# A new order of all pieces in a fused attention and feed-forward block, and output tiles in spent weights

## The chip, the cores and the metric

The kernel runs on one core of a Trainium2 chip. The metric is the device time of one execution in microseconds (us), as a median of several runs. All times of single instructions come from one execution that the hardware profiler recorded.

## The reference

One block of a transformer, on 2,048 rows of 640 values in bf16. A layer normalisation feeds two branches, and their sum is added to the input:

```
xn = layernorm(x)
A:  q, k, v = xn @ wqkv, 32 heads of 20
    row s sees the 8 rows s, s-2, ..., s-14
    logits = q . k * 20**-0.5 ; softmax over the 8 ; o = sum attn * v
    A = o @ wo
B:  B = gelu(xn @ w1 + b1) @ w2 + b2        (w1: 640 x 1536)
out = x + A + B
```

## The kernel before

The rows are worked off in four chunks (n = 0 to 3) of 512 rows, each of four blocks (j or bl = 0 to 3) of 128 rows. Everything is cut into 659 *pieces*, and a list written out by hand, `ORDER` (lines 42 to 74), calls them one after the other (lines 765 and 766) under a manual schedule: each engine and each DMA queue executes its own instructions strictly in the order of the list. So the list sets what waits behind what. Waits between engines and for transfers are put in from what each piece reads and writes.

The names of the pieces, with the chunk as the first digit:

- `xn31` normalises block 1 of chunk 3 (ScalarE), `tc31` transposes it with a DMA of the SP queue into the tile `xnT` of the chunk (`do_td`, line 293). `xnT` holds all four blocks, so a projection needs all four transposes.
- `pj302`: projection to q (second digit 0), k (1) or v (2), fifth 2 of the output (`do_pj`, line 330): five matmuls of 128x512. `pc302` copies the result out of PSUM (ScalarE). In chunk 0 smaller pieces `hj`, `hc` and others do this.
- `qk`: VectorE multiplies q by the shifted k, one block j and one half h of the window at a time, into the tile `half`; `pa` adds parts of it up; `lg` sums over a head with matmuls; `cl` copies the logits (ScalarE); `m`, `mx`, `ex`, `ss`, `ri`, `at` are the softmax (VectorE, `ex` on ScalarE).
- `xd10`: a DMA of the SP queue spreads the softmax of chunk 1, block 0, over the partitions of a head (`do_xd`, line 553), 256 KB. `av100` and `av101` multiply it by the shifted v into the same tile `half` (VectorE). `aa10` adds the two halves with an accumulating DMA of the POOL queue (`do_aa`, line 570), 640 KB; in chunk 3 VectorE adds. `ab10` and `ot10` add further on VectorE, into the tile `oT`.
- `f11_4` and `ge1_4`: one of twelve slices of the first feed-forward matmul (five matmuls) and its gelu (ScalarE).
- `o010` to `o014`: the output of chunk 0, block 1, in five pieces: four of feed-forward slices, three pairs of matmuls each, and the last, five pairs, of `oT` with `wo`. `oc01` copies it to an output tile (ScalarE), `od01` adds that to the output in DRAM (POOL queue, accumulating).
- `xp0`, `xp1`, `xp2` write x to the output (SP queue; blocks 0 to 3, 4 to 7, 8 to 14), `xb0` to `xb3` add b2 to it (POOL queue). `ld2` and `ldo` load w2, and wo with b2.

`half` is one tile for all chunks, so the `av` products of a chunk come after `lg` has read its `qk` products. PSUM tiles for projections and feed-forward rotate through six buffers, normalised blocks through three, output tiles through two. The lines that carry the reads the prediction speaks of:

```
def do_td(n, bl):                                            # line 293
    nc.sync.dma_start_transpose(xnT[:, :, bl * P : (bl + 1) * P], tiles["xn", n, bl][:])
def do_pj(n, which, to):                                     # line 330
    xnT = tiles["xnT", n]
...
            rhs=xnT[:, ti, :],
def do_xd(n, j):                                             # line 553
    nc.sync.dma_start(
        ax_view(n)[:, j, :, :],
def do_aa(n, j):                                             # line 570
        nc.gpsimd.dma_start(a, b, accum_op=ALU.add, max_dma_last_dim=CUT)
```

The queue orders that matter, read off the list. SP before: `... xp0 xp2 ldo ld2 tc23 tc20 tc21 tc22 xd00 xd02 xd01 xd03 xp1 xd10 tc30 xd12 xd13 xd11 tc31 tc33 tc32 xd23 ...`. POOL before: `xb3 xb2 xb0 pad02 aa00 aa02 aa01 od00 aa03 aa10 aa11 aa13 od02 aa12 od01 od03 xb1 od12 ...`.

Of the kernel before, what the change touches and what calls it, by code (L numbers as in the profile page):

```python
# [22 lines left out]
NCH = S // CH  # L23
BPC = CH // P
# [21 lines left out]
st13a st13 hj112 hc112 st10 st12 rs1 qk010 rc1 qk000 qk011 hj110 f10_0 ge0_0 hj212 xn13 qk001 xn10 tc13 xn11 hc212  # L46
pa010 hj011 hj010 hc010 f10_11 f10_2 hc110 hc011 qk031 qk021 ge0_11 f10_10 qk020 pa000 su23 f10_6 xn12 ge0_10 qk030
pa020 su21 tc10 tc11 su22 hj200 hc200 f10_3 ge0_3 pa030 pa011 f10_9 tc12 xp0 su20 ng2 sq21 ge0_9 pa021 pj101 pc101
ge0_2 sq23 pj111 pj102 pj114 pc114 xp2 pc102 pj110 pc110 pj104 pa001 ge0_6 pa031 lg0 pc111 cl0 ldo xb3 xb2 pc104 mask
m0 mx0 ex0 pj112 pj103 pc103 pj113 pc113 ss0 ri0 pad11 pj100 pc100 pc112 qk121 qk120 hj211 sq20 hc211 qk101 ld2 pj124  # L50
qk100 sq22 pc124 f10_4 rs2 f11_6 pj121 rc2 ge0_4 pa120 qk110 f11_2 f10_1 ge0_1 pa121 qk111 xn21 pj123 pc123 ge1_6
pa122 pa100 pa110 xn23 f10_7 ge0_7 f11_8 tc23 f11_0 o000 xn20 tc20 tc21 ge1_2 f10_5 ge1_0 xb0 xn22 tc22 qk131 at0 xd00
ge1_8 f11_3 ge1_3 pa111 qk130 su32 pa101 pc121 f10_8 ge0_8 pad02 hj210 f11_5 pa130 pj120 pc120 pj200 pc200 pa112 pj211
pc211 pj210 pj212 pa131 pa102 pc210 hc210 pad12 pa132 lg1 av000 cl1 pj202 ge0_5 pj214 pc202 pj204 av001 aa00 m1 xd02
av021 pad21 av020 xd01 av011 av010 pj220 pj203 su33 ge1_5 su31 su30 ng3 sq33 xd03 av031 o001 pc212 pc203 o002 pc214
sq30 ab00 ot00 aa02 aa01 sq32 sq31 pj213 pc213 xp1 pj221 pj224 rs3 av030 ab02 pj122 pc122 pad22 rc3 ot02 o003 o004
oc00 od00 pj201 mx1 ex1 ss1 ri1 at1 xn31 pc220 xn30 f11_9 o020 o021 o022 o023 xd10 ab01 ot01 pc204 o024 oc02 pc201
aa03 tc30 ab03 f11_4 pc224 o030 o031 o032 pj223 o033 ot03 o034 xn33 av100 f12_3 av101 aa10 xn32 pc223 xd12 av120 xd13
f12_0 f11_11 av130 oc03 pc221 o010 o011 ge2_3 f12_11 o012 ge2_11 ge1_4 ge1_9 xd11 av110 av111 aa11 o013 o014 av121
pj222 pc222 av131 aa13 tc31 tc33 tc32 pj302 pj322 pj300 pc322 pj314 pc314 pj312 ab10 f11_1 ge1_11 ge1_1 f11_7 pj303  # L60
qk201 ot10 qk200 pa200 pc312 ge2_0 pj301 pc301 ab11 pa201 f11_10 pc302 ge1_10 qk211 ot11 od02 qk210 ab13 qk231 ot13
pj324 pc324 pj304 pc304 pa210 qk230 aa12 qk221 ab12 ge1_7 pj311 pa211 oc01 ot12 pa230 od01 f13_2 qk220 pc311 f12_8
pa212 od03 ge3_2 pa220 pc300 o130 pa231 pj313 pa221 o131 o132 o133 o134 oc13 pj310 f13_0 pc303 pc310 ge2_8 xb1 o120
pa202 pa232 pa222 lg2 o121 o122 pad31 pc313 qk300 f13_6 qk311 cl2 m2 qk310 f13_10 qk331 mx2 ge3_6 f13_8 qk330 ge3_0
f13_3 ge3_3 pa310 o123 qk301 o124 ex2 ss2 oc12 od12 f12_7 qk320 ri2 pa311 at2 xd23 pa330 pa300 qk321 f12_4 o110 o111
o112 pa301 o113 ge3_10 f12_10 pa320 pa312 o114 oc11 ge2_10 f12_6 f13_7 ge3_7 ge3_8 ge2_7 o100 o101 pa321 f12_2 xd21
od13 pa331 pa302 pa322 f12_5 o102 o103 ge2_6 ge2_5 o104 pa332 lg3 od11 oc10 od10 pj323 av210 pc323 av211 f12_9 cl3 m3
f13_1 xd22 xd20 ge3_1 pj321 av230 f12_1 ge2_1 aa21 av231 f13_5 ge3_5 av201 av200 aa23 f13_9 mx3 ge2_2 ge2_4 aa20 ab21
f13_4 ge2_9 ot21 ex3 ss3 ri3 ge3_4 f13_11 ge3_11 av220 ab23 o210 o211 at3 xd30 o212 o213 o214 ot23 oc21 od21 av221
aa22 pj320 o330 ab20 pc321 ot20 ge3_9 pad32 pc320 av300 o310 av301 o200 o201 o202 o203 o204 oc20 od20 o311 o230 o231  # L70
xd31 av310 o232 xd32 o233 o234 oc23 o312 o220 o221 o222 av311 aa31 ab22 ot22 o223 o224 od23 oc22 od22 av321 o313 av320
aa32 ab32 ot32 o320 o321 o322 o323 o324 oc32 od32 ab31 ot31 o314 oc31 od31 o300 xd33 o301 o302 o303 aa30 av331 ab30
ot30 o304 oc30 od30 av330 aa33 ab33 ot33 o331 o332 o333 o334 ohi xl oclo ochi ochd
""".split()


# [1 line left out]
def kernel(  # L78
# [16 lines left out]
    nc = tc.nc  # L95
# [19 lines left out]
    outp = ctx.enter_context(tc.tile_pool(name="outp", bufs=2))  # L115
# [3 lines left out]
    wqkv = [wts.tile([P, KT, D], BF16, name=f"w{s}_sb") for s in "qkv"]  # L119
# [60 lines left out]
    mask = consts.tile([H, W, MW], BF16, name="mask")  # L180
# [283 lines left out]
    def do_pa(n, j, k):  # L464

        a, b = ((slice(0, 2), slice(2, 4)), (slice(0, 1), slice(1, 2)), (slice(0, 1), slice(4, 5)))[k]
        kept, gone = (half[:, j, :, :, ts, :].rearrange("p h w t c -> p (h w) t c") for ts in (a, b))
        if k == 0 and j in PA_DMA[n]:
            nc.gpsimd.dma_start(kept, gone, accum_op=ALU.add)
            return  # L470
        nc.vector.tensor_tensor(out=kept, in0=kept, in1=gone, op=ALU.add)  # L471

    def do_lg(n):
# [102 lines left out]

    def do_ab(n, j):
        a, b = (half[:, j, 0, w : w + 2].rearrange("p w t c -> p (w t c)") for w in (0, 2))
        if j in AB_DMA[n]:
            nc.gpsimd.dma_start(a, b, accum_op=ALU.add)  # L580
        else:
            nc.vector.tensor_tensor(out=a, in0=a, in1=b, op=ALU.add)  # L582
# [33 lines left out]
    def do_o(n, bl, pc, parts):  # L616
# [11 lines left out]
        for k, (lhs, rhs) in enumerate(srcs):  # L628
# [80 lines left out]
    for n in range(NCH):  # L709
# [87 lines left out]
```

## Time and profile before

| | us |
|---|---|
| median of 3 runs | 205.92 (205.92 to 206.48) |
| the profiled execution | 206.31 |
| its span, first to last instruction | 204.5 |
| TensorE busy | 200.3 (98%), 1,261 matmuls |
| VectorE busy | 181.6 (89%) |
| ScalarE busy | 127.2 (62%) |
| granted TensorE clock | 1.000 |

A span is counted from the first instruction of the program to the last; all positions below are us from its start. PE is TensorE, DVE VectorE, ACT ScalarE, SP the engine whose queue issues most transfers, POOL the engine that issues the accumulating ones. Matmuls are pipelined: one of 128x512 is listed with 379 ns but the next starts 216 ns later, so a piece of five takes 1.08 us of PE; a pair of 128x512 and 128x128 takes 0.272. VectorE's long products are listed with 1,483 ns and follow each other every 1.40 us.

### The profile page before, as it was taken

To read this page: it belongs to the slowest core of one execution; us is meant where nothing else is said; L and a number is where in the kernel's file an instruction comes from. 1 tells how busy PE (TensorE), PEld (TensorE's weight loads), DVE (VectorE), ACT (ScalarE), POOL (GpSimd) and SP (SyncE) were. 2 spreads that over 40 slices of the span, in tenths; PEclk is the share of its full clock that TensorE was granted. 3 is DMA by queue.
4 is the path that set the end of the run, shared out by engine and by line. 5 is a ranking of instruction groups with operands and counts; after the bars stand their busy time and mean duration, and the time that the engine had idled before them with its cause. 6 is when DMAs were issued, how large, how long until landed. Compare 5 with 4: busy or idle time off the path is not lost.

```text
span 204.5 us, 3231 instructions
## 1 busy us (share of the span) xinstructions
PE 200.3 (98%) x1261; PEld 111.4 (54%) x1261; DVE 181.6 (89%) x226; ACT 127.2 (62%) x246; POOL 34.6 (17%) x49
## 2 busy tenths in 40 slices
PE   8999999999999999999999999999999999999994
PEld 3898565564464555554554554455554455555552
DVE  2699999499998997877999999999989999889991
ACT  5589999999957998846335825474525793111210
POOL 2000000430000243002260050003104224111120
PEclk9999999999999999999999999999999999999999
DMA  6999469899358399999999086005642997962153
GB/s 208 392 396 380 109 213 328 306 256 199 78 116 275 67 171 163 163 144 151 192 190 189 6 90 105 0 0 69 130 107 32 169 189 127 216 101 25 27 67 64
DMA packets 27335, 31.77 MB, mean 155 GB/s; under 512 B 9272, under 2 KB 22072, under 8 KB 27320
## 3 DMA queue, kind: packets, MB, share of 16 engines
q0 software_dynamic: 7408, 12.78, 39.0%
q1 hardware_dynamic: 19600, 18.58, 31.8%
q8 instruction: 10, 0.16, 0.4%
q10 hardware_dynamic: 312, 0.20, 0.3%
q14 instruction: 5, 0.04, 0.1%
HBM read 10.00 MB, written 7.54 MB: 86 GB/s over the span
## 4 chain that ended last, share of the span: by engine, by line
PE 75%; DVE 15%; DMA 5%; ACT 2%; issue 1%; SPq 1%; DVEq 0%; ACTq 0%
PE lo L631 23%; PE hps L595 20%; PE pps L339 17%; PE gps L383 7%; PE hi L633 6%; DVE half L436 5%; DVE half L471 5%; DMA x_sb<-e 3%; DVE half L563 3%; PE gps L352 1%; DVE half L582 1%; DMA x_sb<-in_A_x_dram 1%; PE L L479 1%; DVE oT L586 1%; PE tp L283 1%
## 5 line engine op out<-in xcount | busy, mean ns | idle before, releaser
L595 PE MATMUL hps<-xnT,w_sb 128*128 128x512 bf16 x240 | 55.6, 379 | 0.0
L436 DVE TENSOR_TENSOR half<-qT,kT 128x2560 bf16<-128x2560 bf16 x32 | 46.6, 1483 | 0.1
L631 PE MATMUL lo<-w_sb,hT 128*128 128x512 bf16 x144 | 41.3, 379 | 0.0
L595 PEld LDWEIGHTS <-w_sb 128*128 128x128 bf16 x240 | 23.1, 98 | 26.2
L471 DVE TENSOR_TENSOR half<-half 128x1024 bf16<-128x1024 bf16 (+1 forms) x44 | 36.5, 878 | 0.0
L638 ACT CAST osb<-lo 128x512 bf16<-128x512 f32 x15 | 8.8, 583 | 37.1 <-PE hi L633 18.3
L633 PE MATMUL hi<-w_sb,hT 128*128 128x128 bf16 x144 | 31.5, 219 | 0.0
L611 ACT ACTIVATE hT<-hps,b1T 128x512 bf16<-128x512 f32 x36 | 24.0, 692 | 6.5 <-PE hps L595 5.6
L563 DVE TENSOR_TENSOR half<-vT,x_sb 128x2560 bf16<-128x2560 bf16 x16 | 23.0, 1487 | 3.3 <-DMA x_sb<-e 3.3
L644 POOL DMA_DIRECT2D out_dram<-osb x15 | 13.7, 959 | 71.8 <-ACT osb L639 71.8
L573 POOL DMA_DIRECT2D half<-half x12 | 15.6, 1302 | 56.1 <-DVE half L563 56.1
L563 DVE TENSOR_TENSOR half<-vT,ax 128x2560 bf16<-128x2560 bf16 x16 | 23.0, 1481 | 1.8 <-PE L L479 1.8
L631 PEld LDWEIGHTS <-hT 128*128 128x128 bf16 x144 | 14.1, 98 | 17.2 <-issue 0.4
L631 PE MATMUL lo<-wo,oT 128*128 128x512 bf16 x80 | 23.1, 379 | 0.0
L339 PE MATMUL pps<-xnT,wq_sb 128*128 128x512 bf16 x75 | 18.5, 379 | 0.0
L339 PE MATMUL pps<-xnT,wv_sb 128*128 128x512 bf16 x75 | 18.3, 379 | 0.0
L339 PE MATMUL pps<-xnT,wk_sb 128*128 128x512 bf16 x75 | 18.0, 379 | 0.0
L633 PE MATMUL hi<-wo,oT 128*128 128x128 bf16 x80 | 16.9, 219 | 0.0
L176 ACT ACT_TABLE_LOAD x12 | 15.4, 1283 | 0.9 <-PEq L781 0.7
L633 PEld LDWEIGHTS <-hT 128*128 128x128 bf16 x144 | 14.1, 98 | 1.9
L582 DVE TENSOR_TENSOR half<-half 128x1280 bf16<-128x1280 bf16 x16 | 13.1, 820 | 0.8 <-DMA half<-half 0.8
L403 ACT CAST vT<-pps 128x512 bf16<-128x512 f32 x15 | 8.8, 587 | 6.9 <-PE pps L339 6.9
(91 smaller groups left out, 262.9 us busy)
## 6 DMA issues: line engine op xcount, KB each, us to landing
half<-half POOLq DMA_DIRECT2D x12, 640.0 KB, 6.9
w_sb<-in_B_w_dram SPq DMA_DIRECT2D x4, 960.0 KB, 11.6
out_dram<-osb POOLq DMA_DIRECT2D x15, 160.0 KB, 3.5
ax<-e SPq DMA_DIRECT2D x8, 256.0 KB, 4.1
x_sb<-e SPq DMA_DIRECT2D x8, 256.0 KB, 4.8
out_dram<-b2bc POOLq DMA_DIRECT2D x3, 640.0 KB, 9.7
x_sb<-in_A_x_dram SPq DMA_DIRECT2D x1, 1280.0 KB, 13.7
out_dram<-x_sb SPq DMA_DIRECT2D x2, 640.0 KB, 4.4
```

Of the source, the lines that this page charges most:

```text
L176: nc.scalar.activation(warm[:], nc.const_aps.tensor(0.0, [P, 1], F32), func)
L339: nc.tensor.matmul(ps[:], lhsT=wqkv_p[which][:, ti, to, :], rhs=xnT[:, ti, :], start=(ti == 0), stop=(ti == KT - 1),)
L383: nc.tensor.matmul(ps[:, to - a, :], lhsT=wqkv_p[which][:, ti, to, :], rhs=tiles["xnT", 0][:, ti, pair * 2 * P : (pair + 1) * 2 * P], star ...
L436: nc.vector.tensor_tensor(out=half[:, j, h], in0=q[:, :, at].unsqueeze(1).to_broadcast([P, W // 2, KT, P]), in1=window(k, h, at), op=ALU.mult,
L471: nc.vector.tensor_tensor(out=kept, in0=kept, in1=gone, op=ALU.add)
L563: nc.vector.tensor_tensor(out=half[:, j, h], in0=window(qkv_tile(n, 2), h, cs), in1=ax_view(n)[:, j, ws, :].unsqueeze(2).to_broadcast([P, ...
L573: nc.gpsimd.dma_start(a, b, accum_op=ALU.add, max_dma_last_dim=CUT)
L582: nc.vector.tensor_tensor(out=a, in0=a, in1=b, op=ALU.add)
L595: nc.tensor.matmul(ps[:], lhsT=w1_sb[:, ti, ft * P : (ft + 1) * P], rhs=tiles["xnT", n][:, ti, :], start=(ti == 0), stop=(ti == KT - 1),)
L611: nc.scalar.activation(hT, tiles["hps", n, ft][:], ACT.Gelu_apprx_tanh, bias=b1T[:, ft : ft + 1], scale=1.0)
L631: nc.tensor.matmul(lo[:], lhsT=lhs, rhs=rhs[:, 0:CH], start=first, stop=last)
L633: nc.tensor.matmul(hi[:, 0 : D - CH], lhsT=lhs, rhs=rhs[:, CH:D], start=first, stop=last)
```

## The change

The list is new from the piece after `st13a` on; the lead-in before it is the same. No piece is added or taken away, and each engine has as many instructions as before. Besides, the output tiles of chunk 3 and of block 0 of chunk 2 no longer come from the two rotating buffers: they lie in the tile of the weights of v (`wqkv[2]`), which no projection reads any more by then. Two options that were empty (`AB_DMA`, `PA_DMA`) are gone with their branches.

Cut to the rows of the list that the prediction speaks of:

```diff
-ge0_2 sq23 pj111 pj102 pj114 pc114 xp2 pc102 pj110 pc110 pj104 pa001 ge0_6 pa031 lg0 pc111 cl0 ldo xb3 xb2 pc104 mask
...
-pc211 pj210 pj212 pa131 pa102 pc210 hc210 pad12 pa132 lg1 av000 cl1 pj202 ge0_5 pj214 pc202 pj204 av001 aa00 m1 xd02
-av021 pad21 av020 xd01 av011 av010 pj220 pj203 su33 ge1_5 su31 su30 ng3 sq33 xd03 av031 o001 pc212 pc203 o002 pc214
-sq30 ab00 ot00 aa02 aa01 sq32 sq31 pj213 pc213 xp1 pj221 pj224 rs3 av030 ab02 pj122 pc122 pad22 rc3 ot02 o003 o004
-oc00 od00 pj201 mx1 ex1 ss1 ri1 at1 xn31 pc220 xn30 f11_9 o020 o021 o022 o023 xd10 ab01 ot01 pc204 o024 oc02 pc201
-aa03 tc30 ab03 f11_4 pc224 o030 o031 o032 pj223 o033 ot03 o034 xn33 av100 f12_3 av101 aa10 xn32 pc223 xd12 av120 xd13
-f12_0 f11_11 av130 oc03 pc221 o010 o011 ge2_3 f12_11 o012 ge2_11 ge1_4 ge1_9 xd11 av110 av111 aa11 o013 o014 av121
-pj222 pc222 av131 aa13 tc31 tc33 tc32 pj302 pj322 pj300 pc322 pj314 pc314 pj312 ab10 f11_1 ge1_11 ge1_1 f11_7 pj303
...
+hc110 hc011 qk000 qk030 tc10 qk021 qk020 f10_11 ge0_11 f10_3 f10_10 xn11 tc11 su22 hj200 xn12 tc12 xp1 ldo f10_9 xp0
+xb0 ge0_3 pa000 pa010 hc200 ge0_10 su20 f10_2 ge0_2 ge0_9 su23 su21 ng2 f10_6 ge0_6 ld2 qk031 sq23 pa020 pj114 pj101
...
+pa131 tc20 pj200 ge0_4 pc200 pa102 pj212 xp2 pj211 pj210 su30 pc212 su32 ng3 sq33 pa132 lg1 pj202 av000 pc202 xd03
+pc210 cl1 av001 sq30 pj203 xd02 av020 aa00 sq31 av021 pc211 aa02 pj201 av031 av011 av010 aa01 pj122 pj213 pj223 pc201
+o001 ab00 ot00 pc213 sq32 rs3 rc3 pj221 av030 xn33 pj204 pj214 pc214 m1 aa03 pad21 pc223 o002 o003 o004 oc00 ab02 od00
+mx1 ex1 f12_3 pj222 pc222 o020 o021 o022 o023 ot02 o024 oc02 ss1 ri1 at1 pc204 ab01 ot01 xn31 f12_11 o030 xn30 o031
+o032 o033 ab03 pc122 xd13 ot03 av130 pc203 o034 f12_8 xd10 av101 av100 oc03 tc33 pad22 o010 xn32 f12_0 ge2_0 xd11
+av110 xd12 av121 aa10 av111 ge2_11 pad31 tc30 aa11 f11_9 ge2_3 av131 aa13 tc31 od02 pc221 o011 o012 o013 o014 av120
+ab10 ge2_8 tc32 pj313 pj303 pc303 pj300 pj322 pc322 qk201 ot10 qk200 aa12 pj220 pj310 pc310 pj304 ab11 pc300 pc313
...
+    def out_tile(n, bl):
+        if (n, bl) == (2, 0) or n == NCH - 1:
+            return wqkv[2][:, bl if n == NCH - 1 else BPC, :]
+        return outp.tile([P, D], BF16, tag="osb", name="osb")
     def do_oc(n, bl):
-        osb = outp.tile([P, D], BF16, tag="osb", name="osb")
+        osb = out_tile(n, bl)
...
     def do_oclo():
-        osb = outp.tile([P, D], BF16, tag="osb", name="osb")
+        osb = out_tile(*last)
```

The queue orders after. SP: `... xp1 ldo xp0 ld2 xd01 xd00 tc21 tc22 tc23 tc20 xp2 xd03 xd02 xd13 xd10 tc33 xd11 xd12 tc30 tc31 tc32 xd22 ...`. POOL: `xb0 pad02 aa00 aa02 aa01 aa03 od00 aa10 aa11 aa13 od02 aa12 od01 od03 xb1 od13 xb2 od12 xb3 od11 ...`.

More of the change, by code (lines that the diff above doesn't have):

```diff
@@ L34 @@
 BY_DMA = ((0, 1, 2, 3), (0, 1, 2, 3), (0, 1, 2, 3), ())
-AB_DMA = ((), (), (), ())
-PA_DMA = ((), (), (), ())
 CUT = 2560
@@ L45 @@
 hc100 xn03 tp03 tc03 pk hj202 rc02 xn02 tp02 tc02 gc4 hj201 hc201 hj111 st11a st10a hc111 st12a hj012 hc012 st11 hc202
-st13a st13 hj112 hc112 st10 st12 rs1 qk010 rc1 qk000 qk011 hj110 f10_0 ge0_0 hj212 xn13 qk001 xn10 tc13 xn11 hc212
-pa010 hj011 hj010 hc010 f10_11 f10_2 hc110 hc011 qk031 qk021 ge0_11 f10_10 qk020 pa000 su23 f10_6 xn12 ge0_10 qk030
-pa020 su21 tc10 tc11 su22 hj200 hc200 f10_3 ge0_3 pa030 pa011 f10_9 tc12 xp0 su20 ng2 sq21 ge0_9 pa021 pj101 pc101
-ge0_2 sq23 pj111 pj102 pj114 pc114 xp2 pc102 pj110 pc110 pj104 pa001 ge0_6 pa031 lg0 pc111 cl0 ldo xb3 xb2 pc104 mask
@@ L50 @@
[L50 to L53, printed above, removed]
-pc211 pj210 pj212 pa131 pa102 pc210 hc210 pad12 pa132 lg1 av000 cl1 pj202 ge0_5 pj214 pc202 pj204 av001 aa00 m1 xd02
@@ L60 @@
-pj222 pc222 av131 aa13 tc31 tc33 tc32 pj302 pj322 pj300 pc322 pj314 pc314 pj312 ab10 f11_1 ge1_11 ge1_1 f11_7 pj303
[L61 to L73, printed above, removed]
+st13a st10 hj112 hc112 hj212 st12 st13 qk001 rs1 rc1 f10_0 ge0_0 xn10 qk011 hj011 qk010 hj010 xn13 tc13 hc010 hj110
@@ new lines @@
+hc110 hc011 qk000 qk030 tc10 qk021 qk020 f10_11 ge0_11 f10_3 f10_10 xn11 tc11 su22 hj200 xn12 tc12 xp1 ldo f10_9 xp0
+xb0 ge0_3 pa000 pa010 hc200 ge0_10 su20 f10_2 ge0_2 ge0_9 su23 su21 ng2 f10_6 ge0_6 ld2 qk031 sq23 pa020 pj114 pj101
+pj111 pc111 pad02 pa001 pa030 pc114 pc101 pj112 pc112 pj104 pa021 sq21 pj110 pc110 pa011 hc212 pa031 lg0 cl0 mask m0
+pc104 mx0 ex0 ss0 ri0 pj100 pc100 pj103 pj102 pc102 pj113 f10_4 hj210 pc113 pc103 pad11 qk121 qk101 qk110 sq22 at0
+sq20 xd01 hc210 xd00 rs2 pj123 pc123 f11_0 ge1_0 rc2 qk120 qk130 f11_6 ge1_6 qk100 qk111 pa100 pj121 pa110 xn21 pc121
@@ new lines @@
+tc21 xn22 tc22 f10_8 ge0_8 pa120 pa111 pa121 xn20 pj120 qk131 pa112 f10_7 pc120 ge0_7 xn23 f11_3 tc23 f11_8 ge1_8
+f11_5 ge1_5 pa130 f10_1 ge0_1 pa101 su33 su31 hj211 hc211 pad12 f10_5 ge0_5 o000 ge1_3 pj124 f11_2 ge1_2 pc124 pa122
+pa131 tc20 pj200 ge0_4 pc200 pa102 pj212 xp2 pj211 pj210 su30 pc212 su32 ng3 sq33 pa132 lg1 pj202 av000 pc202 xd03
+pc210 cl1 av001 sq30 pj203 xd02 av020 aa00 sq31 av021 pc211 aa02 pj201 av031 av011 av010 aa01 pj122 pj213 pj223 pc201
+o001 ab00 ot00 pc213 sq32 rs3 rc3 pj221 av030 xn33 pj204 pj214 pc214 m1 aa03 pad21 pc223 o002 o003 o004 oc00 ab02 od00
@@ new lines @@
+mx1 ex1 f12_3 pj222 pc222 o020 o021 o022 o023 ot02 o024 oc02 ss1 ri1 at1 pc204 ab01 ot01 xn31 f12_11 o030 xn30 o031
+o032 o033 ab03 pc122 xd13 ot03 av130 pc203 o034 f12_8 xd10 av101 av100 oc03 tc33 pad22 o010 xn32 f12_0 ge2_0 xd11
+av110 xd12 av121 aa10 av111 ge2_11 pad31 tc30 aa11 f11_9 ge2_3 av131 aa13 tc31 od02 pc221 o011 o012 o013 o014 av120
+ab10 ge2_8 tc32 pj313 pj303 pc303 pj300 pj322 pc322 qk201 ot10 qk200 aa12 pj220 pj310 pc310 pj304 ab11 pc300 pc313
+pj301 pc301 f11_10 pa200 ge1_10 pc220 ot11 pc304 qk211 qk210 ab13 f11_11 pj302 f13_2 ge3_2 pc302 f11_4 pa210 ge1_4
@@ new lines @@
+pj224 oc01 pc224 f13_0 od01 ot13 qk231 qk230 od03 ab12 pa211 f11_1 ge1_1 qk221 ot12 pa230 pj312 pj311 pc311 qk220
+f11_7 pa201 ge1_7 o130 pj314 pa220 pa202 pc312 ge1_9 pa231 pa221 ge1_11 o131 o132 o133 o134 oc13 xb1 od13 pad32 pj324
+pc324 pa212 o120 xb2 pa222 pa232 lg2 pc314 qk300 f12_10 qk320 o121 cl2 m2 mx2 ex2 ge2_10 qk331 o122 o123 o124 oc12
+f12_4 ge2_4 f13_6 qk310 qk321 qk311 f13_7 ss2 ri2 f12_5 od12 pa310 pa320 o110 f12_2 f13_8 ge3_8 pa311 o111 o112 qk330
+o113 o114 oc11 f12_7 o100 ge3_6 at2 xd22 qk301 xd21 pa321 o101 o102 pa300 pa330 pa322 ge2_2 ge2_7 f13_10 pa301 o103
@@ new lines @@
+xb3 f12_6 ge2_6 o104 pa331 ge3_7 pa312 pa302 ge2_5 od11 oc10 od10 f13_3 ge3_3 pa332 lg3 av210 f13_11 cl3 f12_9 ge3_11
+av211 f13_4 ge3_4 ge3_10 m3 f13_5 xd23 av230 av231 f12_1 ge2_1 xd20 av200 f13_1 ge3_1 mx3 pj323 av201 ge3_0 pc323 aa21
+ab21 ot21 av220 pj320 o310 ge3_5 o330 ex3 ss3 ge2_9 pj321 pc321 o210 o211 o212 o213 ri3 at3 xd30 av221 xl aa23 aa20
+aa22 o214 oc21 od21 ab20 ot20 f13_9 ab23 pc320 o200 o201 o202 o203 o204 oc20 av300 o311 o230 o231 o232 o233 ot23 o234
+oc23 od20 o312 av301 xd31 av310 av311 aa31 o220 o221 o222 ab22 ot22 o223 o224 od23 ge3_9 o313 oc22 xd32 av321 av320
@@ L74 @@
+o320 o321 o322 o323 aa32 ab32 od22 ot32 o324 ab31 ot31 o314 aa30 ab30 ot30 oc32 od32 oc31 od31 xd33 av330 av331 aa33
+ab33 ot33 o300 o301 o302 o303 o304 oc30 od30 o331 o332 o333 o334 oclo ohi ochi ochd
 """.split()
@@ L467, in do_pa @@
         kept, gone = (half[:, j, :, :, ts, :].rearrange("p h w t c -> p (h w) t c") for ts in (a, b))
-        if k == 0 and j in PA_DMA[n]:
-            nc.gpsimd.dma_start(kept, gone, accum_op=ALU.add)
-            return
         nc.vector.tensor_tensor(out=kept, in0=kept, in1=gone, op=ALU.add)
@@ L578, in do_ab @@
         a, b = (half[:, j, 0, w : w + 2].rearrange("p w t c -> p (w t c)") for w in (0, 2))
[L579 to L582, printed above, removed]
+        nc.vector.tensor_tensor(out=a, in0=a, in1=b, op=ALU.add)
     def do_ot(n, j):
```

## The prediction

> **What bounds the kernel now.** I read the busy shares first, then TensorE's waits, then the chain, then the timelines of the queues. The page:
>
> ```profile
> PE 200.3 (98%) x1261; PEld 111.4 (54%) x1261; DVE 181.6 (89%) x226; ACT 127.2 (62%) x246; POOL 34.6 (17%) x49
> PE   8999999999999999999999999999999999999994
> DMA  6999469899358399999999086005642997962153
> PE 75%; DVE 15%; DMA 5%; ACT 2%; issue 1%; SPq 1%; DVEq 0%; ACTq 0%
> ```
>
> TensorE never rests between its first microseconds and its last. A busy PE proves little, so I took the gaps between starts: outside the lead-in only one place is more than a quarter of a microsecond over the usual step, the logits of chunk 2. The timeline of PE there:
>
> ```profile
> 127.13 0.39 PE L479 MATMUL L<-half,head_of 128*32 128x512 bf16 x2
> 127.70 0.61 PE L479 MATMUL L<-half,head_of 128*32 128x512 bf16 x6 [0.18 <-DVE half L471]
> ```
>
> Two starts 0.57 us apart instead of 0.06: PE waited 0.51 us for VectorE's last addition. So the chain crosses to VectorE and to DMA (15% and 5%) only because both run neck and neck with PE up to here. The kernel is bound by TensorE, and an order alone can win at most this 0.51 us. It can lose wherever PE is sent to something that is not there yet. The two places to look at are VectorE's and the DMAs'. The timelines of SP and POOL around the only stretch where DMA is full for long (slices 14 to 21, 72 to 112 us), with what is known of the last two transposes:
>
> ```profile
> 85.31 0.55 SPq L554 DMA_DIRECT2D x_sb<-e  x1
> 85.97 2.12 SPq L295 DMA_TRANSPOSE xnT<-xn  x1
> 88.18 2.66 SPq L554 DMA_DIRECT2D x_sb<-e  x3
> 90.89 7.97 SPq L295 DMA_TRANSPOSE xnT<-xn  x3
> ...
> 92.57 1.20 POOL L573 DMA_DIRECT2D half<-half  x1 [10.55 <-DVE half L563]
> 99.64 1.20 POOL L573 DMA_DIRECT2D half<-half  x1 [5.87 <-DVE half L563]
> ...
> DMA to landing us min/median/max: 4.6/6.1/7.6
> ...
> 94.00:96.00 2.00, 2.00 (x13) 0.94 (x11) 1.16 (x1) 1.18 (x3) 0.00 (x0) 1.00 1.45 54
> 96.00:100.00 4.00, 4.00 (x29) 2.11 (x27) 3.55 (x3) 2.25 (x4) 0.36 (x1) 1.00 1.03 190
> ...
> 101.10 1.24 PE L339 MATMUL pps<-xnT,wv_sb 128*128 128x512 bf16 x5
> 102.18 0.59 PE L339 MATMUL pps<-xnT,wq_sb 128*128 128x512 bf16 x2
> ```
>
> The landing row is for the transposes issued at 93.3 and 96.85: 7.6 us after the first (100.9) and 4.6 us after the second (101.4). The two rows by windows end with the DMA share and GB/s: from 94 to 96 the engines hold packets and move a quarter of what they do after. The last row is `pj302`, the first projection of chunk 3, which needs all four transposes: it found them with 0.8 us to spare.
>
> **The change part by part.** Each engine has the same instructions, the twelve table loads of ScalarE included, so nothing is added up but waits. The sum is made against the profiled execution (206.31: span 204.5 and 1.8 around it); it lies 0.39 above the median, and I put the difference on the median, 205.92.
>
> *PE's places.* With 1.08 us for a slice or projection and 0.272 for a pair of output matmuls, I added up what stands ahead of each point in both lists. The four logits, `o004`, `o204` and `o334` come out at the same microsecond (35.5, 64.5, 127.2, 152.9, 77.4, 173.8, 199.4 in both). What moved lies between them. The first projection of chunk 3 moved most. Before, `f11_11`, `f11_4`, `pj220` and `pj224` stood ahead of it and now do not; `f12_8` was behind and is ahead. That is three pieces less: PE comes to `pj313` at 102.18 - 3 x 1.08 = 98.94.
>
> *The four transposes of chunk 3.* They wait on SP behind the first spread of chunk 1, and that behind the softmax. Is the softmax earlier? Its exponential starts at 81.02 once ScalarE has copied `o004` and loaded a table (copies 78.85 and 79.33, load 79.61). Both stand as before, and VectorE's `mx1` ends about 80.1, which is soon enough: the shuffle of VectorE's pieces gains nothing, and the spread is issued at 85.3 again. Then SP sends the same eight transfers, four spreads and four transposes, one transpose early and three last in both lists. In the profile that took until 101.4. Bounds: in an idle stretch (52 to 59 us) each of four transposes landed 2.4 us after its issue; the last can't be issued before `xn32`, which follows the copy of `o034` on ScalarE (91.3 + 0.7 + 0.2 for `pad22` + 0.9 = 93.1), so 95.5 at best, no wait. At worst they share the engines with all four accumulations of chunk 1 and land with the third of these, about 107. I take 101.4, the row of this very set of transfers. PE then starts `pj313` about 0.1 us after it (at the logits VectorE's addition ended at 127.65 and PE went on at 127.70), at 101.5: a wait of 2.56 us. PE has no idle time behind it to win this back.
>
> *VectorE up to the logits of chunk 2.* Its idle times before: 1.46 (exponential), 0.26 (`ab03`), 1.23 and 1.29 (spreads). Now `ot02` stands ahead of the wait for the exponential but ends in the same 82.1; `aa03` is issued right behind `av030`, no longer behind `od00`, so 0.26 goes; the first spread is awaited until 89.4 as before; the third is issued earlier, so 1.29 may go. But the product that completes the first accumulation is third, not second, so `aa10` is issued at 93.8, not 92.57; with the 7.8 us it took, `ab10` starts about 101.6 instead of 102.06. Then the same 25.5 us of work: the last addition ends by 127.2, while PE comes to `lg2` at 127.13 + 2.56. So the 0.51 us goes. VectorE then waits for the copy of `pj314` (it stands on ScalarE behind that of `o134`, which PE ends at 125.1 + 2.56; four copies of 1.8 us in all follow) and starts chunk 3's products at about 129.6; 25.0 us later (127.63 to 152.60 before) it has the last addition at 154.6, against PE at `lg3` at 153.26 - 0.51 + 2.56 = 155.3. No further wait, but the margin is 0.7.
>
> *The rest, at nothing, with its cover.* Moving `xb2` and `xb3` from 39 us behind `xb1` (126 us on) puts 1.1 MB beside the spreads of chunk 2; these landed at 152 at the latest and the products start at 153.7. The spreads `xd01`, `xd00` go ahead of the transposes of chunk 2 (softmax done at 47.7), the last of which then is issued at 56.4 (`xn23` is ready at 55.0 in ScalarE's new order) and lands 2.4 us later, 1.3 before PE wants `pj200` (60.1). `xp2` now stands on SP ahead of `xd03` and `xd02`: it and two spreads are the same 1.6 MB that landed in 9.0 us from 58.26, so from 57.6 by 66.6, and `av020` comes at 67.9; a delay below 0.9 would be hidden under ScalarE's table load. The tile change: before, an output copy had to wait for the landing two blocks earlier, but the waits of line 638 end with PE (18.3 and 8.9 us) or with nothing shown, never with a DMA, and the closest landing (196.3) lies 1.5 us ahead of its copy (197.8); so nothing is gained, and no projection to v is left that could be hurt. After `lg3`, VectorE's results come 1.3 us or more ahead of PE's use. PSUM is freed at the nearest 0.2 us ahead, as before.
>
> Sum: 205.92 + 2.56 - 0.51 = 207.97, so **208.0**.
>
> [...] While `aa10` moves, I counted the trace's DMA packets: in 97 to 99 us 79 and 64 of 2,560 bytes a microsecond, and beside them only 71 and 69 of a transpose's 256 bytes; right behind, from 100.0, 991 of these passed in 0.93 us. [...]
>
> **The rivals.**
> *Crawl.* The pass in the gap between `aa10` and `aa11` is what let the transposes land by 101.4: these two were issued 7.07 us apart. Now three products lie between them (3 x 1.40 = 4.2 us), and an accumulation's packets take 3.6 us (96.41 to 99.98), so the gap is 0.6 us or none. Three transposes are 1,920 packets; 525 had passed by 94.6, and at the rate of issue (640 in 1.2 us) some 700 more do by 95.6, where `aa10` now starts. Beside it 407 passed, so some 300 are left for the next accumulation: landing at 103.5 to 107, about 105, a wait of 6.1. Time: 205.92 - 0.51 + 6.1 = 211.5. Against it: 300 packets need no more than a gap of 0.3 us.
> *Hidden (the other side, not slower).* `aa10` starts 1.2 us later, and at 991 packets in 0.93 us the 1,920 need 1.8 us. It decides if the last lands before 98.9. Then only 0.51 is left: 205.4. Against it: SP needed 2.0 to 3.5 us to issue each of the three, and the standstill of 94 to 96 may recur.
> *VectorE's margin.* A late `xd02` or the 0.7 at `lg3` give 0.2 to 1.0 more on any case.
>
> **How the numbers follow.** A change below 0.3% (0.6 us) can't be told from none. The forecast (206.6 to 210) has 0.50, crawl (over 210) 0.22, hidden 0.25 (205.3 to 206.5, mostly same), a run below 205.3 0.03, since the floor is 205.41. The forecast's own range is 206.6 to 210. Four in five lie from 205.2, the floor with its scatter, to 212.5, inside the crawl. Faster 0.03, same 0.23, slower 0.74.
>
> **What would show it.** The profile after should have PE idle before line 339's first chunk-3 matmul, near 99 us, ended by the DMA `xnT<-xn`; no gap at `lg2`; VectorE idle near 127 to 130, before a product of q and k; the spread issued at 85.3. I am wrong if the transposes land before 98.9, if the softmax of chunk 1 is earlier, or if PE has a second gap: at `pj200`, at `lg3`, or where a product is waited for.

## The result and the profile after

The changed kernel takes 209.11 us in the median (208.31 to 209.88, 6 runs), beside 205.94 for the kernel before on the same chip: 1.0152 times, 95% interval 1.0136 to 1.0168. The profiled execution took 209.24 (span 207.2), 2.93 more than that of before. The forecast, 208.0, was 1.1 us short, with the right sign and the time inside its range. Executions at a lower granted clock, or more than 1.5% above the fastest of the same kernel, are left out of all ratios.

The page of the changed kernel: busy shares, TensorE and DMA by slices, the chain by engines.

```profile
PE 199.1 (96%) x1239; PEld 111.2 (54%) x1261; DVE 181.4 (88%) x226; ACT 126.7 (61%) x246; POOL 34.6 (17%) x49
...
PE   8899999999999999999699999999999999999994
...
DMA  6999399983867299899997093738382997972253
...
PE 77%; ACT 10%; DMA 8%; issue 2%; DVE 1%; SPq 0%; another core or an unknown queue 0%; ACTq 0%
```

Slice 20 (98 to 104 us) has a 6 where before had a 9: TensorE stood still there. (22 records of matmuls are missing from this trace: a group that shows x4 where a piece has five is such a hole, and the busy share can't be set against that of before.) The chain has lost VectorE, 15% before and 1% now, and has ScalarE at 10%. From the list of waits (engine, line, waited for: total, times, longest):

```profile
DVE half L434 <- PE L L474: 3.9, 1, 3.9
...
PE pps L337 <- DMA xnT<-xn: 1.7, 1, 1.7
...
ACT xn L264 <- DMA xnT<-xn: 0.9, 1, 0.9
...
PE hps L587 <- ACT hT L603: 0.7, 1, 0.7
```

And the timelines of the changed kernel at those places (start, length, what; in brackets the idle time before it and what ended it):

```profile
55.73 0.92 ACT L264 ACTIVATE xn<-x_sb,nmr,rstd 128x640 bf16<-128x640 bf16 x1 [0.93 <-DMA xnT<-xn]
...
57.28 1.24 PE L587 MATMUL hps<-xnT,w_sb 128*128 128x512 bf16 x4 [0.68 <-ACT hT L603]
...
86.44 1.19 SPq L549 DMA_DIRECT2D x_sb<-e  x2
87.75 2.01 SPq L293 DMA_TRANSPOSE xnT<-xn  x1
89.80 1.24 SPq L549 DMA_DIRECT2D x_sb<-e  x2
91.14 5.75 SPq L293 DMA_TRANSPOSE xnT<-xn  x3
...
94.89 1.20 POOL L568 DMA_DIRECT2D half<-half  x1 [12.97 <-DVE half L558]
99.10 1.19 POOL L568 DMA_DIRECT2D half<-half  x1 [3.01 <-DVE half L558]
...
100.11 0.22 PE L625 MATMUL hi<-wo,oT 128*128 128x128 bf16 x1
102.04 1.25 PE L337 MATMUL pps<-xnT,wk_sb 128*128 128x512 bf16 x4 [1.71 <-DMA xnT<-xn]
...
130.23 0.61 PE L474 MATMUL L<-half,head_of 128*32 128x512 bf16 x8
130.73 2.90 DVE L434 TENSOR_TENSOR half<-qT,kT 128x2560 bf16<-128x2560 bf16 x2 [3.88 <-PE L L474]
```

Read by TensorE's starts, beyond the usual step: 1.88 us before `pj313` (100.1 to 102.0), where the forecast put 2.56; no wait inside the eight logits of chunk 2, where before had 0.51; and 0.84 before `f10_5` at 57.28, which the forecast did not have. That one starts on ScalarE: `xn23` waited until 55.7 for a transpose, its buffer being one of three, and the gelu behind it (`ge1_8`) held the PSUM buffer that `f10_5` takes. With 0.39 in the unchanged lead-in (first weights landed 0.38 later in this execution) the sum is 0.39 + 0.84 + 1.88 - 0.51 = 2.60 of a span that is 2.7 longer.

### The profile page after: what moved, and what is told of

Its sections match the earlier page's. It is cut to its first block, busy times and chain, and to the rows that moved or that the text cites. A ratio compares the mean times of both kernels' runs of the same rounds, so it can differ in the third digit from the quotient of the medians.

```text
span 207.2 us, 3202 instructions
## 1 busy us (share of the span) xinstructions
PE 199.1 (96%) x1239; PEld 111.2 (54%) x1261; DVE 181.4 (88%) x226; ACT 126.7 (61%) x246; POOL 34.6 (17%) x49
## 4 chain that ended last, share of the span: by engine, by line
PE 77%; ACT 10%; DMA 8%; issue 2%; DVE 1%; SPq 0%; another core or an unknown queue 0%; ACTq 0%
PE lo L623 24%; PE pps L337 20%; PE hps L587 18%; PE hi L625 7%; DMA xnT<-xn 6%; PE gps L381 6%; DMA wq_sb<-in_A_wqkv_dram 3%; ACT xn L264 2%; ACT L174 1%; PE gps L350 1%; ACT qT L401 1%; ACT hT L603 1%; PE L L474 1%; ACT trash L229 1%; ACT osb L635 1%
## 5 line engine op out<-in xcount | busy, mean ns | idle before, releaser
L623 PE MATMUL lo<-w_sb,hT 128*128 128x512 bf16 x140 | 40.5, 379 | 0.1
L466 DVE TENSOR_TENSOR half<-half 128x1024 bf16<-128x1024 bf16 (+1 forms) x44 | 35.8, 876 | 0.0
L568 POOL DMA_DIRECT2D half<-half x12 | 15.1, 1258 | 65.1 <-DVE half L558 62.9
L635 ACT CAST osb<-lo 128x512 bf16<-128x512 f32 x11 | 6.4, 585 | 22.4 <-PE lo L623 13.0
L641 POOL DMA_DIRECT2D out_dram<-osb x11 | 10.8, 1009 | 53.4 <-ACT osb L636 44.7
L337 PE MATMUL pps<-xnT,wq_sb 128*128 128x512 bf16 x72 | 17.6, 380 | 0.2
L337 PEld LDWEIGHTS <-wk_sb 128*128 128x128 bf16 x75 | 8.6, 118 | 9.3 <-issue 2.4
```

The source lines that it names most:

```text
L337: nc.tensor.matmul(ps[:], lhsT=wqkv_p[which][:, ti, to, :], rhs=xnT[:, ti, :], start=(ti == 0), stop=(ti == KT - 1),)
L623: nc.tensor.matmul(lo[:], lhsT=lhs, rhs=rhs[:, 0:CH], start=first, stop=last)
```

## The experiments

Theory: the new order loses at two places, where `xn23` waits for a buffer and where PE comes three pieces too early for the last transpose of chunk 3. Rivals: the loss is given back elsewhere, belongs to the tiles, or is DMA time that no order sets. Ratios are to the kernel before on the same chip, with 95% intervals.

**One cure: `xn23` in a buffer of its own.**

```diff
     def xn_tile(n, bl):
+        if (n, bl) == (2, 3):
+            return get(("xn", n, bl), lambda: outp.tile([P, D], BF16, tag="osb", name="xn23"))
         return get(("xn", n, bl), lambda: lnp.tile([P, D], BF16, tag="xn", name="xn"))
```

> The changed kernel, but the last normalised block of chunk 2 (`xn23`) gets a tile of its own (an output buffer that is not yet used at 55 us), so it no longer shares a buffer with the block whose transpose `tc21` landed at 55.65. Theory (the 0.84 us that PE stood still before `f10_5` came from ScalarE waiting in `xn23` for that landing): `xn23` starts near 54.8, the gap at 57 us goes, everything behind it, the first spread of chunk 1 included, comes some 0.6 to 0.8 us earlier, and the time is 209.1 - 0.7 = 208.4. Rival 1 (given back): the gap goes, but the last transpose of chunk 3 does not land earlier, so PE waits 0.7 us longer at `pj313`: 209.1. Rival 2 (another cause): the gap before `f10_5` stays at 0.8: 209.1.

Measured: 208.63, ratio 1.0102 (1.0068 to 1.0136). In its timeline ScalarE goes into `xn23` without idle time, although `tc21` landed as late as before (55.85), and PE has no gap at `f10_5`:

```profile
54.88 0.94 ACT L266 ACTIVATE xn<-x_sb,nmr,rstd 128x640 bf16<-128x640 bf16 x1
```

So the buffer was the cause, and the time is 0.2 us from the expected 208.4. The wait at `pj313` stayed (1.39). The first rival falls: the last transpose came earlier by as much as PE, and more.

**The other cure: three pieces ahead of `pj313`.**

```diff
-ab10 ge2_8 tc32 pj313 pj303 pc303 pj300 pj322 pc322 qk201 ot10 qk200 aa12 pj220 pj310 pc310 pj304 ab11 pc300 pc313
-pj301 pc301 f11_10 pa200 ge1_10 pc220 ot11 pc304 ...
-pj224 oc01 pc224 ...
+ab10 ge2_8 tc32 pj220 pc220 f11_10 ge1_10 pj224 pc224 pj313 pj303 pc303 pj300 pj322 pc322 qk201 ot10 qk200 aa12 pj310
```

> The changed kernel with six pieces (`pj220` and its copy, `f11_10` and its gelu, `pj224` and its copy: 3 x 1.08 us of PE work that needs no transpose of chunk 3) moved from behind `pj313` to in front of it. Theory (PE came three pieces too early for the last transpose, nothing more): the wait at `pj313` (1.88) goes, since PE comes there at 103.4 with the landing at 101.9; the gap before `f10_5` stays; time 209.1 - 1.9 = 207.2. Rival (the wait only moves: the projections that now stand right behind wait for the transposes or for PSUM buffers, or VectorE, which gets chunk 3's projections no earlier, ends later): a gap of 1 us or more at another place behind 101 us, time 208.5 to 209.1.

Measured: 207.78, ratio 1.0084 (1.0047 to 1.0120). The timeline goes from one projection into `pj313` (line 337, `wk_sb`) with no idle time:

```profile
101.98 1.24 PE L337 MATMUL pps<-xnT,wv_sb 128*128 128x512 bf16 x5
103.06 1.24 PE L337 MATMUL pps<-xnT,wk_sb 128*128 128x512 bf16 x5
```

The transpose landed at 101.78, as before the cure; no new gap appears, and that at `f10_5` is still there (0.77). The profiled execution, 206.96, is where the theory put it (207.2); the median is 0.6 above the theory.

**The same step in the old list.** Three pieces go from in front of chunk 3's first projection to behind it; nothing else of the change is in.

```diff
-f12_0 f11_11 av130 oc03 pc221 o010 o011 ge2_3 f12_11 o012 ge2_11 ge1_4 ge1_9 xd11 av110 av111 aa11 o013 o014 av121
-pj222 pc222 av131 aa13 tc31 tc33 tc32 pj302 pj322 pj300 pc322 pj314 ...
+f12_0 av130 oc03 pc221 o010 o011 ge2_3 o012 ge1_4 ge1_9 xd11 av110 av111 aa11 o013 o014 av121
+av131 aa13 tc31 tc33 tc32 pj302 pj322 pj300 pc322 f11_11 f12_11 ge2_11 pj222 pc222 pj314 ...
```

> The kernel before, with five pieces (`f11_11`, `f12_11` and its gelu, `pj222` and its copy: 3 x 1.08 us of PE work) moved from in front of the first projections of chunk 3 to behind them, so that PE comes to `pj302` at 98.9 instead of 102.18; nothing else of the change. Theory (the wait at chunk 3's first projection is the price of three pieces less in front): PE waits there for the last transpose (landing 101.4) for 2.5 us, the 0.51 us at the logits of chunk 2 goes, time 205.9 + 2.5 - 0.5 = 207.9. Rival (hidden): the transposes land earlier too or the wait is won back, 205.4 to 206.2.

Measured: 210.11, ratio 1.0187 (1.0146 to 1.0227). The timeline:

```profile
99.16 0.22 PE L633 MATMUL hi<-wo,oT 128*128 128x128 bf16 x1
102.58 0.60 PE L339 MATMUL pps<-xnT,wq_sb 128*128 128x512 bf16 x2 [3.20 <-DMA xnT<-xn]
```

PE came 3.4 us too early, and the 0.51 at the logits went. The step alone costs as much as the whole change (the intervals overlap), since the transpose landed at 102.49 here and not at 101.41. Hidden it is not. But the expected 207.9 was missed by 2.2 us: 0.9 of it is the longer wait, and 0.7 lies between the profiled execution (209.39) and the median.

**The tiles alone, the order alone.** The first is the old list with `out_tile`, the second the new list with the old line:

```diff
 # the order alone
-        osb = out_tile(n, bl)
+        osb = outp.tile([P, D], BF16, tag="osb", name="osb")
```

> The old list of pieces with the new place of the output tiles (chunk 3 and block 0 of chunk 2 in the spent weights of v). Theory (an output copy ends with PE, not with the landing of an earlier output): the same time as before, 205.9 within 0.4. Rival (the tiles save waits for landings, or make copies wait for the last projections to v): 0.5 us or more away from before, on either side.

> The new list of pieces with the old two rotating output tiles. Theory (the whole difference is the order): the changed kernel's time, 209.1 (1.012 to 1.018 times before), with the gaps at `f10_5` (0.8) and `pj313` (1.9). Rival (the new order needs the new tiles, since outputs of chunk 2 and 3 follow each other faster in it): 209.6 or more, with ScalarE's output copies ended by DMA landings near 150 or behind 195 us.

Measured: tiles alone 206.19, ratio 1.0006 (0.9988 to 1.0023), no difference. Order alone 210.74, ratio 1.0240 (1.0211 to 1.0268): the rival holds. It is slower than with the new tiles, and the theory (209.1) is wrong. Its timeline has a third gap:

```profile
184.84 0.58 ACT L638 CAST osb<-lo 128x512 bf16<-128x512 f32 x1 [6.54 <-DMA out_dram<-osb]
...
185.47 0.38 PE L631 MATMUL lo<-w_sb,hT 128*128 128x512 bf16 x1 [1.67 <-ACT osb L638]
```

The copy `oc23` waits until an earlier output has landed, and PE waits 1.83 us for the copy before `o220`. So the tiles are worth nothing in the old order and 1.8 us in the new one.

**Both cures.**

> The changed kernel with both cures: a tile of its own for `xn23`, and three pieces of PE work (`pj220`, `f11_10`, `pj224` with their copies and gelu) ahead of `pj313`. Theory (the two waits are the whole loss, and the 0.51 us at the logits of chunk 2 is a true gain): no gap over 0.3 us behind the lead-in, 205.4 to 206.0, that is 0.997 to 1.000 times before. Rival (something that no gap of PE shows, or a new wait, holds the changed order back): 206.8 or more, as the two single cures, which came out 0.3 to 0.6 us less well than their gaps, would let one think.

Measured: 206.84, ratio 1.0036 (1.0020 to 1.0052). The profiled execution, 206.10 with a span of 204.2, has no gap of PE over 0.3 behind the lead-in, and its chain is:

```profile
PE 95%; DMA 1%; ACT 1%; issue 1%; DVE 0%
```

That execution has the theory's time within 0.1 us. The other eleven lie between 206.45 and 208.35, and the median is the rival's (206.8 or more). So the two waits are most of the loss (1.0152 to 1.0036), and about 0.7 us stays that this profile does not show.

**Where does the time of the transposes go?** In the trace a 16 KB packet of the queue called instruction passes ten times, about once per 250 PE instructions (weight loads and matmuls). At 26, 53 and 95 us one fell among the 256-byte packets of transposes; there 19, 22 and 17 of these were under way at once for 1 to 2 us each, and little else moved (35 GB/s in 27 to 28, 36 in 54 to 55, 57 in 95 to 96). Such packets are called held below, and the stretch a hold. The stretches 52 to 56 of the changed kernel (engine columns, granted clock, then DMA share and GB/s), with this packet at 53.14:

```profile
52.00:53.00 1.00, 1.00 (x7) 0.42 (x5) 1.00 (x2) 1.00 (x3) 0.00 (x0) 1.00 1.17 205
53.00:54.00 1.00, 1.00 (x6) 0.45 (x5) 1.00 (x1) 1.00 (x2) 0.00 (x0) 1.00 2.26 90
54.00:55.00 1.00, 1.00 (x6) 0.47 (x5) 1.00 (x2) 0.81 (x2) 0.00 (x0) 1.00 0.22 36
```

The packets that start in 53 to 54 fill the DMA engines 2.26 times over while 90 GB/s pass, then 36. If this is what made `tc21` late, moving the packet must move the hold. Three kernels move it by idle matmuls in the warm-up, whose results nothing reads:

```diff
         do_warm(3, P)
+        do_warm(12, 32)     # on the kernel after; and on the kernel before
...
-        do_warm(WARM, CH)
+        do_warm(WARM - 4, CH)
         do_warm(3, P)
+        do_warm(40, 32)     # on the kernel after, the longer one
```

> The changed kernel with 12 more idle matmuls of 32 columns in the warm-up ahead of the first piece, where PE waits for its first weights anyway; nothing else is touched. In the trace a 16 KB packet of the instruction queue passes once per some 256 PE instructions; at 53.14 and at 94.73 it fell among the 256-byte packets of transposes, and at both places some 20 packets of all engines then took 1 to 2 us. 24 more PE instructions bring these packets some 2 us earlier (near 51 and 92.7), where only 2,048-byte packets are under way. Theory (the instruction packet among the transposes holds the DMA engines): no packet is held near 53 and near 95, `tc21` lands near 54 instead of 55.65 and the gap before `f10_5` goes (0.7), `tc32` lands 1 us or more earlier against PE's course, so that the wait at `pj313` falls from 1.9 to under 1: 207.0 to 208.0. Rival (the hold belongs to the transposes, or to the start of an accumulation, or is chance): holds at the same places as before, time 209.1 within 0.3.

> The kernel before with 12 more idle matmuls of 32 columns in the warm-up and nothing else; it asks where the instruction packets fall, not for time. Theory (an instruction packet among 256-byte packets of transposes holds the DMA engines for 1 to 2 us): if the packet at 93.76 moves out of the transposes, no packets are held near 94 to 96, and the transposes issued at 93.3 and 96.85 land 1 us or more before 100.9 and 101.4; if it moves onto other transposes (those of chunk 2, 53 to 59 us), the hold appears there. The time stays (205.9 within 0.4), for PE did not wait for them. Rival (the hold belongs to the start of the first accumulation): held near 94 to 96 wherever the packet falls.

> The changed kernel with a longer warm-up in front of the first piece (6 idle matmuls of 512 columns in place of 10, and 40 of 32 columns): some 72 more PE instructions, which should bring each packet of the instruction queue some 7 us earlier, to about 46 and 88 in place of 53 and 95, both ahead of transposes. Theory (an instruction packet among transposes holds the DMA engines): no packets are held near 53 nor near 95; `tc21` takes 3.3 us in place of 4.6 and the gap before `f10_5` goes; `tc32` lands 1.5 us sooner after its issue, at 5 to 5.7 in place of 7.2, and the wait at `pj313` falls below 1.0. Time 207.0 to 207.8, plus what the longer warm-up costs in the lead-in (0 to 0.5). Rival (the hold near 95 belongs to the transposes or to the first accumulation): it stays, with a wait of 1.4 to 2.1 at `pj313`, and the time is 208.3 to 209.3.

Measured. Twelve matmuls on the kernel after: ratio 1.0123 (1.0048 to 1.0197), so nothing follows from the time. The packet went from 53.1 to 47.6, no packets were held there, `tc21` took 3.25 us in place of 4.57, and the gap at `f10_5` was gone; but the later packet stayed among the transposes (95.3), and so did the hold. (Its profile is of an execution of 211.53 us; the kernel with forty repeats what it shows at 53.) Twelve on the kernel before: ratio 1.0020 (1.0004 to 1.0035); the packet at 93.8 did not move, nor the hold: inconclusive for its question. Forty: 208.92 and 208.98 us, two of four executions, without a ratio; the rival's time. Both packets moved, to 44.8 and 90.0. The same stretch as above now reads:

```profile
52.00:53.00 1.00, 1.00 (x7) 0.47 (x5) 1.00 (x1) 1.00 (x2) 0.00 (x0) 1.00 0.83 183
53.00:54.00 1.00, 1.00 (x7) 0.41 (x6) 1.00 (x2) 1.00 (x2) 0.00 (x0) 1.00 0.92 175
54.00:55.00 1.00, 1.00 (x6) 0.49 (x5) 1.00 (x2) 1.00 (x3) 0.00 (x0) 1.00 0.74 167
```

The hold at 53 is gone and with it the gap at `f10_5`, without touching a buffer; the hold at 95 is gone too; and a new one stands at 90.3 to 90.8, among the packets of `tc33`, which took 5.0 us in place of 4.2. So the hold follows the packet, and it is what made `tc21` late. Its price at `pj313` was misjudged, though: that wait stayed at 2.03, and `tc32`, with no packet held, still took 6.1 us. Something else sets its landing.

**What sets the landing of the last transpose.** Read from the traces (us):

```
kernel                       aa10 issued  landed    tc32 issued  landed
before                          92.57     100.33       96.85     101.41
after                           94.89     101.34       94.70     101.90
xn23 in a buffer of its own     94.32     100.72       94.36     100.89
both cures                      93.76     100.09       93.77     100.09
old list, three behind          92.83     101.42       94.83     102.49
forty idle matmuls              95.19     101.33       95.73     101.82
aa10 behind aa11               100.48     109.30       95.86      99.35
```

In all rows but the last, `tc32` lands 0 to 1.1 us behind `aa10`, whenever it was issued (4.6 to 7.7 us before it lands). The packets of the changed kernel show how: in 98 to 100 us 57 and 67 of the transpose's packets a microsecond passed beside 72 and 72 of the accumulation's, 156 of its 640 up to 100.42; once the last packet of `aa10` had started then, the other 484 passed in 0.98 us. The last row is the test, one issue moved on POOL:

```diff
-av110 xd12 av121 aa10 av111 ge2_11 pad31 tc30 aa11 f11_9 ...
+av110 xd12 av121 av111 ge2_11 pad31 tc30 aa11 aa10 f11_9 ...
```

> The changed kernel with one issue on POOL moved: the first accumulation of chunk 1 (`aa10`) behind the second (`aa11`), so that both start near 99 to 101 us and none runs while the last transposes of chunk 3 do. It asks when `tc32` lands. In all traces so far the last transpose lands 0 to 1.2 us behind `aa10` (90 to 102 us: landings 100.1 to 103.4), whether it was issued 2.5 or 7.4 us earlier, and whether packets were held or not. Theory (the last transpose goes packet for packet beside `aa10` and so ends with it): without it `tc32` lands 2.4 to 4.5 us after its issue, at 97.2 to 99.3, PE finds it there and the wait at `pj313` (1.9) goes. VectorE then waits for `aa10` until about 107, some 5 us, and PE for VectorE at the logits of chunk 2, by 2 to 4 us: time 209 to 211. Rival (held packets, or the transposes' own rate, set the landing): `tc32` lands at 101 or later as before, wait 1.4 to 2.0 at `pj313`, time 211 to 213.

Measured: 214.82, ratio 1.0386 (1.0322 to 1.0450). `tc32` landed 3.5 us after its issue though packets were held in its way (16, behind the instruction packet at 95.8), and PE went into `pj313` without a wait. How long the last two transposes took to land in the changed kernel and in this one, the timeline of PE and VectorE, and the stretches behind the waits (granted clock third from the end):

```profile
DMA to landing us min/median/max: 4.0/5.6/7.2
...
DMA to landing us min/median/max: 3.5/3.8/4.2
...
100.85 0.22 PE L624 MATMUL hi<-wo,oT 128*128 128x128 bf16 x1
100.91 1.24 PE L336 MATMUL pps<-xnT,wk_sb 128*128 128x512 bf16 x4
...
109.39 0.82 DVE L573 TENSOR_TENSOR half<-half 128x1280 bf16<-128x1280 bf16 x1 [7.11 <-DMA half<-half]
...
131.77 0.38 PE L473 MATMUL L<-half,head_of 128*32 128x512 bf16 x1 [2.61 <-DVE half L465]
133.58 0.38 PE L473 MATMUL L<-half,head_of 128*32 128x512 bf16 x1 [1.43 <-DVE half L465]
...
134.00:136.00 2.00, 1.40 (x6) 0.34 (x7) 2.00 (x3) 0.59 (x2) 0.00 (x0) 0.60 0.83 138
136.00:138.00 2.00, 1.87 (x5) 0.70 (x5) 1.97 (x4) 1.97 (x3) 0.00 (x0) 0.54 0.00 0
138.00:140.00 2.00, 2.00 (x17) 1.12 (x15) 1.93 (x4) 0.74 (x1) 0.00 (x0) 1.00 0.00 0
```

The theory on the landing holds. The time is above what it gave, and above the rival's too: VectorE waited 7.1 us for the late accumulation, not 5; PE stood idle 4.5 us at the logits of chunk 2; and right behind these waits the granted clock was 0.60 and 0.54, with matmuls of 128x512 every 427 ns in place of 216. From the last output matmul ahead of the logits to the first one behind them PE took 8.89 us, beside 1.79 in the changed kernel. With 7.1 for that, 0.5 in the lead-in and the 1.88 gone at `pj313`, the sum is 5.7 of a span that is 5.8 longer.

**Two tries at a faster kernel.** Both cures with the longer warm-up, and the old list with one output piece ahead of the logits that waited:

```diff
-pa202 pa232 pa222 lg2 o121 o122 pad31 pc313 ...
+pa202 pa232 pa222 o121 lg2 o122 pad31 pc313 ...
```

> The changed kernel with both cures (own tile for `xn23`, three pieces ahead of `pj313`) and the longer warm-up. The two cures alone came out at 206.84, 0.7 us above what their profile (206.1, no gap of PE) says. Theory (in the other executions the held transposes come later still and PE waits after all): without holds the median falls to the profile's level, 205.8 to 206.3. Rival (the 0.7 has nothing to do with held packets): 206.7 to 207.3.

> The kernel before with one piece moved: `o121` (three pairs of output matmuls, 0.81 us of PE work that waits for nothing) stands ahead of the logits of chunk 2 and no longer behind them. Theory (the 0.51 us in those logits is the only wait of PE behind the lead-in that an order can remove): PE has the 0.51 us of work in hand, the softmax starts 0.3 us later, which nothing waits for; 205.4 to 205.7, 0.9965 to 0.9985 times before. Rival (the softmax of chunk 2, 0.3 us later, is what chunk 2's spreads and VectorE's products wait for up to `lg3`, where the gain is given back): 206.0 to 206.4, with a gap of 0.3 to 0.5 at `lg3`.

Measured: 207.02, ratio 1.0046 (1.0029 to 1.0063), and 206.99, ratio 1.0058 (1.0038 to 1.0078). The first speaks against the idea that the packets held near 53 and 94 make the 0.7 us of the two cures: both holds are gone from its profile (one of 17 packets stands at 89.3), and the median is no better. The second was to win 0.5 and lost. Its logits of chunk 2 have no wait, but those of chunk 3 have two:

```profile
14.49 1.68 DVE L211 BATCH_NORM_STATS2 stats<-x_sb 128x6 f32<-128x320 bf16 x4 [1.54 <-DMA x_sb<-in_A_x_dram]
...
154.25 0.55 PE L478 MATMUL L<-half,head_of 128*32 128x512 bf16 x3
155.03 0.59 PE L478 MATMUL L<-half,head_of 128*32 128x512 bf16 x5 [0.23 <-DVE half L470]
155.55 0.63 PE L338 MATMUL pps<-xnT,wv_sb 128*128 128x512 bf16 x2
```

From the first of these logits to the next piece PE took 1.30 us, beside 0.55 for the same eight without a wait and 1.12 for those of chunk 2 in the kernel before: 0.57 was won there and 0.75 lost here. So VectorE takes the whole gain back 25 us later, as its rival said. The time is above the rival's too (206.0 to 206.4), and the rest of the loss was not found. The profiled execution alone has another 1.39 us at 29 us, ahead of anything that was edited; it begins with the input x, for which VectorE waited until 14.49 (first line). No version beat the kernel before.

## Why the prediction was right, and where it was not

*The bound.* Right. Every gap that mattered was TensorE waiting, and with both waits cured the profiled span came to 204.2, beside 204.5 before. The 0.51 us at the logits of chunk 2 went, as forecast (0.57, measured from the first logit to the next piece).

*PE's place at `pj313`.* Right. The count of three pieces gave 98.94; the trace has 100.16, later by the 1.2 us that PE had lost before (0.39 and 0.84). Taking the three pieces back removes the wait; moving three pieces in the old list makes it.

*The landing of the last transpose.* The size was near, in part by luck, for the reason was not right. The text took 101.4 because the same eight transfers had taken until then; measured 101.90. But it is not the set of transfers that ends there: it is the first accumulation, and the last transpose lands with it. So what the counted row had shown of the old list (71 and 69 packets of a transpose a microsecond beside 79 and 64 of the accumulation), which the text kept for a rival, was at work in the main case (57 and 67 beside 72 and 72): `tc32` ended beside `aa10` whether it had 4.6 or 7.7 us for it, and 3.5 us after its issue without it. How the DMA engines choose between the two queues is not shown. The crawl was priced too high, by its own objection: the gap between the last packet of `aa10` and the first of `aa11` (100.42 to 101.02) was the 0.6 us that the text gave it, 291 packets of `tc32` passed in it, and the last 193 by 101.40. The wait came out at 1.88 and not 2.56, since PE was 1.2 us late and the landing only 0.5.

*"The rest, at nothing, with its cover."* This is the step that failed. Of the transposes of chunk 2 the text asked only whether the last would land before `pj200`, and it does (60.4 beside 61.3). It took `xn23` to be ready "at 55.0 in ScalarE's new order" and left out that this block needs the buffer that `tc21` reads, and that `tc21`, now behind two spreads and with an instruction packet in its way, would take 4.6 us and not 2.4. Missed term: 0.84 us. Measured by its cure, about 1 us (ratio 1.0152 to 1.0102, intervals that just touch). That the sum still came within 1.1 us is partly luck: the 0.84 that it missed and the 0.68 by which it made the wait at `pj313` too long nearly cancel.

*The tiles.* The term, nothing, came out right for the sum by luck. The text argued from the old order that no output copy waits for a landing; in the new order one would, and cost 1.8 us, had the tiles not been changed with it.

*VectorE.* Right in size: idle from 126.9 to 130.7 before chunk 3's products, awaited from 127 to 129.6, and no wait at `lg3`. By the profile what ended that idle time was not the copy of `pj314`, as the text had it, but the logits of chunk 2, whose tile `half` the product writes over (`<-PE L L474` in the timeline of the result); the copy had ended 0.1 us earlier, at 130.60. The spread was issued at 86.4 and not at 85.3: the softmax is no earlier, and PE's 1.2 us stand ahead of it.

*What stays open.* The kernel with both cures is 0.36% slower than before in the median, while its profiled execution is not; the cause of that difference was not found. One place that no experiment looked at is the first projection of chunk 1, near 29 us. In the old list it starts 0.73 to 0.77 us after its last transpose has landed (four of five traces). In the changed kernel it is 0.13, and 0.13 to 0.14 is what is left where PE does wait there: 0.28 us with `xn23` in its own buffer and 0.32 with `aa10` behind `aa11`. With both cures it is 0.36, so the new order has little in hand there for a later landing. That this is the 0.7 us is not shown; with both cures and the longer warm-up it is 0.88, and the median is no better.

## What to carry to other kernels

The last transpose landed 0 to 1.2 us behind the longer transfer beside it on another queue in thirteen traces, and 3.5 us after its issue without that one; so a landing in such company is better read from the neighbour's end than from its own issue. When an order changes, each rotating buffer (normalised blocks, output tiles, PSUM) has to be walked through again in the new order: a wait that the old trace does not show proves nothing for the new one. And a wait cured by moving work is worth its length only if the next engine's margin is longer, which the 0.6 us won and lost again at the logits shows.

## What was not expected of the hardware

Over the fourteen traces, the two kernels and twelve experiments, 32 instruction packets (16 KB) fell among transposes, with over 200 packets of 256 bytes from 0.5 us before to 1.5 us behind them. Behind 28 of them 11 to 25 packets at once took more than 0.9 us. The four without a hold lie near 25 us, all in the old list. Behind the 108 others there was no such hold; one hold (98.6 us, in the kernel with `o121` moved) had no instruction packet ahead of it. Moving the packet by idle matmuls moved the hold. What the packets (16,384 bytes, ten in about 2,500 PE instructions) carry is not shown. TensorE itself was not seen to wait at them: in the kernel before its starts lie at most 0.31 us apart behind the lead-in, but for 0.57 at the logits of chunk 2, where no such packet passed (118.3 and 139.6 are the nearest). What came late are the transposes beside them: `tc21` took 4.57 us with the packet at 53.1 and 3.25 with it at 47.6.

In two traces the granted clock stood at 0.5 for 3.41 us right behind a wait of TensorE: from 134.41 with `aa10` behind `aa11`, and from 102.84 with twelve idle matmuls on the kernel after, behind 2.1 us at `pj313` (ten matmuls then took 3.85 us in place of 2.16). The waits of 1.9, 2.0 and 3.4 us at the same place, in the changed kernel, with forty idle matmuls and in the old list with three behind, had no such stretch behind them. So the price of a wait can be more than its length, and its length alone did not decide it here.
